# Fused attention and feed-forward kernel: q and k of a head pair normed into one tile and transposed on the chip, with a new model behind the order of instructions

## The chip, the cores and the metric

The kernel runs on one core of a Trainium2 chip. The metric is device time in microseconds (us), from the first to the last instruction of the slowest core (here the only one) as timed without a profile. A profile of one execution is read beside it. Its engines are PE (TensorE matmul), PEld (TensorE weight load), DVE (VectorE), ACT (ScalarE), POOL (GpSimd) and SP (SyncE, which only issues DMA here).

## The reference

Two parts, one after the other. First an attention with RMS-normed q and k (8 batches, 12 heads, 448 positions, head dimension 64), then a feed-forward with the activation h * erf(softplus(h)):

```python
batch, n_heads, seq, head_dim = (8, 12, 448, 64)
def rmsnorm(x, g):
    rms = np.sqrt(np.mean(x * x, axis=-1, keepdims=True) + 1e-06)
    return x / rms * g
q_n, k_n = (rmsnorm(q, g_q), rmsnorm(k, g_k))
scores = (1.0 / np.sqrt(64)) * np.matmul(q_n, k_n.transpose(0, 1, 3, 2))
attn = softmax(scores)                      # over the last axis
attn_out = np.matmul(attn, v)
x = attn_out.transpose(0, 2, 1, 3).reshape(8 * 448, 768)
h = x @ w_in                                # 768 x 2048
sp = softplus(h)
out = (h * erf(sp)) @ w_out                 # 2048 x 768, float32 result
```

(The softmax and softplus are written out in the original; inputs and output are float32.)

## The kernel before

Heads are handled in pairs (two heads of 64 make 128 partitions), six pairs per batch, 48 in all. The kernel does not issue instructions as it goes. It collects operations in a list (`add(engine, cost, due, function, reads, writes, ...)`), orders them by a small model of the engines (`Plan.order`), and emits them in that order. Engines take their own instructions strictly in that order on the chip. The engine letters are P (TensorE), V (VectorE), A (ScalarE), G (GpSimd) and S (SyncE); "VA" means whichever of the two the model finds free.

The path of q and k, batches 1 to 7: load a unit of 4 heads, square on GpSimd, sum on VectorE, 1/rms on ScalarE, scale by it on VectorE to bf16, store to DRAM, and read back transposed, one pair at a time:

```python
    qn_d = [dram.tile([S, d_model], BF16, name=f"qn{b}") for b in range(B)]
    kn_d = [dram.tile([S + D, d_model], BF16, name=f"kn{b}") for b in range(B)]
    ...
    def add_norm(b, a_key):
        for g, units in enumerate(((0, 1, 2, 3), (4, 5, 6))):
            ...
                add("G", 1.5, tg + i, ... nc.gpsimd.tensor_tensor(sq, raw, raw, op=ALU.mult) ...)
                add("V", 0.95, tg + i, ... nc.vector.tensor_reduce(ss[:, i, :], sq, axis=AX.X, op=ALU.add) ...)
            ...                                     # ACT: Ln, then Exp(-0.5 x)
                add("V", 0.96, tg + 8 + i, norm, ... writes=[("qkn", m)])
                for dst, src, dks in unit_stores(qkn, b, u):
                    add("S", 0.5, tg + 10 + i, ... nc.sync.dma_start(dst, src), reads=[("qkn", m)], writes=dks, ...)
    ...
    def add_pair_inputs(b, p):
        if b or p >= N_PET:                         # N_PET = 2
            for nm, dst, src in (("kT", kTs[m], kn_d), ("qT", qTs[m], qn_d)):
                add("S", 1.3, t0 - 14, ... nc.sync.dma_start(
                    dst, src[b][:, p * P : (p + 1) * P], transpose=True), ...)
            def scale():
                nc.vector.tensor_scalar_mul(kps[kp][0:D, 0:S], kTs[m][0:D, D : S + D], gcomb[0:D])
                nc.vector.tensor_scalar_mul(kps[kp][D:P, S : 2 * S], kTs[m][D:P, 0:S], gcomb[D:P])
            add("V", 0.7, t0 - 6, scale, ...)
```

Batch 0 is normed pair by pair; its first two pairs are transposed by TensorE (14 transposes of 128 x 128 in all) and the other four go through DRAM as well. `kp` holds the two heads' scaled keys in the two halves of the partitions, with zeros in the other half, so that a score matmul over all 128 rows gives one head's scores. Attention of one pair: seven score matmuls of 448 columns, four exponentials, eight value matmuls into one PSUM tile `o` with two halves, then Ln, Ln and Exp for the reciprocal of the sum, and two multiplies into `xT`:

```python
    o_ps = ps.tile([P, 2, 512], F32, name="o")
    ...
    add("P", 0.189, ... nc.tensor.matmul(st[:, i, :S], kk[:, c0 : c0 + P], qq, start=True, stop=True) ...)
    add("A", 0.925, ... nc.scalar.activation(e, st[:, :, :S], func=FN.Exp) ...)
    add("P", 0.189, ... nc.tensor.matmul(o_ps[:, half, :S], lhs, rhs, start=(s == 0), stop=(s == 3)) ...)
    ...
    add("V", 0.62, ... nc.vector.tensor_tensor(x[0:D, p, :], o_ps[0:D, 0, :S], r[0:D], op=ALU.mult) ...)
    add("V", 0.62, ... nc.vector.tensor_tensor(x[D:P, p, :], o_ps[D:P, 1, :S], r[D:P], op=ALU.mult) ...)
```

The feed-forward of a batch follows while later batches are in attention: the first product (`f <- xT, w_in_sb`, 96 matmuls of 448 columns, copied to `h` by VectorE or ScalarE), then on ScalarE a block of four Softplus and four Erf with three loads of function tables, then the products h * erf on VectorE, then the second product (`f <- g, w_out_sb`, 96 or 128 matmuls of 384 columns). The block of batch b-1 stands behind all of ScalarE's attention work of batch b:

```python
    for b in range(B):
        if b:
            add_ffn1(b - 1)
        for p in range(NP):
            ...                                     # attention of pair p, inputs of pair p + 1
        if b > 1:
            add_ffn2(b - 2)
        if b:
            add_act_block(b - 1, act_ops(i0))
    add_ffn1(B - 1); add_ffn2(B - 2); add_act_block(B - 1, []); add_ffn2(B - 1)
```

Of the kernel before, what the change touches and what calls it, by code (L numbers as in the profile page):

```python
# [10 lines left out]
F32 = mybir.dt.float32  # L11
# [6 lines left out]
class Op:  # L18
    __slots__ = ("eng", "cost", "lat", "work", "due", "fn", "idx", "need", "users", "ready", "start", "end", "took", "sync", "inst")


class Plan:
# [5 lines left out]
    SLACK = {"P": 0.3, "V": 0.15, "A": 0.1, "G": 0.2, "S": 0.2}  # L28
# [4 lines left out]
    def add(self, eng, cost, due, fn, reads=(), writes=(), lat=0.0, after=(), work=0.0, sync=()):  # L33
# [3 lines left out]
        o.sync = sync  # L37
# [19 lines left out]
    def order(self):  # L57
        free = {e: 0.0 for e in self.SLACK}
        avail = {e: [] for e in self.SLACK}
        future = [(0.0, o.idx) for o in self.ops if not o.need]  # L60
        heapq.heapify(future)
        now, out, dma, lanes = 0.0, [], {}, ([], [])
        while len(out) < len(self.ops):
            while future and future[0][0] <= now + 1e-9:
                o = self.ops[heapq.heappop(future)[1]]
                for i, e in enumerate(o.eng):
                    heapq.heappush(avail[e], (o.due if i == 0 else 1e9 + o.due, o.idx))
            for e, h in avail.items():
                while h and self.ops[h[0][1]].took:
                    heapq.heappop(h)  # L70
                if h and free[e] <= now + 1e-9:
                    o = self.ops[heapq.heappop(h)[1]]
                    o.took, o.start = e, now
                    o.end = now + (o.cost if type(o.cost) is float else o.cost[e])
                    if o.work:
                        done = lanes[e == "G"]
                        if len(done) >= 8:
                            o.end += max(0.0, done[-8] - now)
                    free[e] = o.end
                    out.append(o)  # L80
                    there = o.end
                    if o.work:
                        t0 = max(dma.get(e, 0.0), o.end)
                        busy = max([0.0] + [t for e2, t in dma.items() if e2 != e]) - t0
                        there = dma[e] = t0 + o.work + min(o.work, max(busy, 0.0))
                        done.append(there + o.lat)
                    for u in o.users:
                        u.need -= 1
                        gap = o.lat + (0.0 if u.eng == e and not o.lat else self.SLACK[u.eng[0]])
                        u.ready = max(u.ready, there + gap)  # L90
                        if not u.need:
                            heapq.heappush(future, (u.ready, u.idx))
            nxt = [free[e] for e, h in avail.items() if h and free[e] > now + 1e-9]
            if future:
                nxt.append(future[0][0])
            if len(out) < len(self.ops):
                now = max(now + 1e-6, min(nxt))
        return sorted(out, key=lambda o: (o.start, o.idx))
# [3 lines left out]
def kernel(  # L102
# [26 lines left out]
    dram = ctx.enter_context(tc.tile_pool(name="dram", bufs=1, space=bass.MemoryType.DRAM))  # L129
# [6 lines left out]
    N_RAW, N_SQ, N_QKN, N_ST, N_QT, N_KP, N_V = 4, 1, 2, 2, 3, 2, 4  # L136
    N_VL, N_E, N_EM, N_R, N_X, N_H, N_O = 2, 5, 2, 2, 2, 5, 3
# [4 lines left out]
    raws = ring(sb, N_RAW, [P, 12, D], F32, "raw")  # L142
    sqs = ring(sb, N_SQ, [P, 12, D], F32, "sq")
    sts = ring(sb, N_ST, [P, 4, 12], F32, "st")
    qkns = ring(sb, N_QKN, [P, 12, D], BF16, "qkn")
    s0s = ring(sb, N_ST, [P, 14], F32, "s0")
    qTs = ring(sb, N_QT, [P, S], BF16, "qT")
    kTs = ring(sb, N_QT, [P, S + D], BF16, "kT")
    kps = ring(sb, N_KP, [P, 2 * S], BF16, "kp")
    vms = ring(sb, N_V, [P, 3, 3 * D], BF16, "vm")  # L150
    vls = ring(sb, N_VL, [P, 2, 3, D], F32, "vl")
    vss = ring(sb, N_VL, [P, D], F32, "vs")
# [6 lines left out]
    sps = ring(sb, NC, [P, 4, S], F32, "sp")  # L159
    gms = [ring(sb, NC, [P, 4, 384], BF16, f"g{i}_") for i in range(2)]  # L160
# [5 lines left out]
    o_ps = ps.tile([P, 2, 512], F32, name="o")  # L166
    f_ps = ring(ps, 2, [P, 512], F32, "f")
    qn_d = [dram.tile([S, d_model], BF16, name=f"qn{b}") for b in range(B)]
    kn_d = [dram.tile([S + D, d_model], BF16, name=f"kn{b}") for b in range(B)]
# [3 lines left out]
    PAIR, BATCH = 9.0, 54.0  # L173
# [4 lines left out]
    for half in range(2):  # L178
        for j, g in enumerate((g_q, g_k)):
            add("G", 0.6, -60, lambda half=half, j=j, g=g: nc.gpsimd.dma_start(  # L180
                ggtmp[half * D : (half + 1) * D, j : j + 1], g[:, None]), writes=[("gg", half, j)], lat=2.0)
    add("V", 0.1, -10, lambda: nc.vector.scalar_tensor_tensor(
        out=gcomb, in0=ggtmp[:, 0:1], scalar=8.0, in1=ggtmp[:, 1:2], op0=ALU.mult, op1=ALU.mult),
        reads=[("gg", a, c) for a in range(2) for c in range(2)], writes=["gcomb"])
    for i in range(N_KP):
        add("V", 0.15, -9, lambda t=kps[i]: nc.vector.memset(t[0:D, S : 2 * S], 0.0), writes=[("kp0", i)])
        add("V", 0.15, -9, lambda t=kps[i]: nc.vector.memset(t[D:P, 0:S], 0.0), writes=[("kp1", i)])
    for i in range(N_V):
        def ones(vm=vms[i], vx=vxs[i]):
            nc.vector.memset(vm[:, :, D : 2 * D], 1.0)  # L190
            nc.vector.memset(vx[0:D, 0, D:P], 1.0)
            nc.vector.memset(vx[D:P, 0, :], 0.0)
            nc.vector.memset(vx[0:D, 1, :], 0.0)
            nc.vector.memset(vx[D:P, 1, 0:D], 1.0)
        add("V", 0.5, -8, ones, writes=[("v1", i)])
    add("G", 1.0, -50, lambda: make_identity(nc, ident), writes=["ident"])
    add("A", 1.3, FIRST, lambda: nc.scalar.preload_act_table_set(LN_EXP), writes=["table"])
# [7 lines left out]
    def unit_loads(t, b, u):  # L205
        if u == 0:
            return [(t[0:D], q[b, :, 384:448, :].rearrange("h p d -> p h d")),
                    (t[D:P], k[b, :, 384:448, :].rearrange("h p d -> p h d"))]
        src, h0 = (q, k)[(u - 1) % 2], (u - 1) // 2 * 4
        return [(t.rearrange("p (h j) d -> p h (j d)", j=3),  # L210
                 src[b, h0 : h0 + 4, 0:384, :].rearrange("h (p j) d -> p h (j d)", j=3))]

    def unit_stores(t, b, u):
        t = t.rearrange("p a d -> p (a d)")
        if u == 0:
            return [(qn_d[b][0:D], t[0:D], [("qn", b, 0, hg) for hg in range(3)]),
                    (kn_d[b][0:D], t[D:P], [("kn", b, 0, hg) for hg in range(3)]),
                    (kn_d[b][S : S + D], t[D:P], [("kn", b, 2, hg) for hg in range(3)])]
        dst, nm, hg = (qn_d, kn_d)[(u - 1) % 2], ("qn", "kn")[(u - 1) % 2], (u - 1) // 2
        return [(dst[b][D:S, hg * 256 : hg * 256 + 256].rearrange("(j p) c -> p j c", p=P),  # L220
                 t.rearrange("p (j c) -> p j c", j=3), [(nm, b, 1, hg)])]

    nu = [0]

    def add_norm(b, a_key):
        for g, units in enumerate(((0, 1, 2, 3), (4, 5, 6))):
            tg = BATCH * (b - 1) + 15 * g + (15 if b == 1 else 0)
            si = nu[0] % N_ST
            nu[0] += 1
            ss, n = sts[si], len(units)  # L230
            sks = [("st", si, i) for i in range(n)]
            def bufs(u):
                i = 7 * b + u
                return i % N_RAW, i % N_SQ, i % N_QKN
            for i, u in enumerate(units):
                r, m, _ = bufs(u)
                raw, sq = raws[r], sqs[m]
                rks = [("raw", r, part) for part in range(2)]
                for part, (dst, src) in enumerate(unit_loads(raw, b, u)):
                    add("S", 0.5, tg - 15 + i, lambda dst=dst, src=src: nc.sync.dma_start(dst, src),  # L240
                        writes=rks[part : part + 1] if u == 0 else rks, lat=1.6, work=0.9 if u == 0 else 1.3)
                add("G", 1.5, tg + i, lambda sq=sq, raw=raw: nc.gpsimd.tensor_tensor(  # L242
                    sq, raw, raw, op=ALU.mult), reads=rks, writes=[("sq", m)])
                add("V", 0.95, tg + i, lambda sq=sq, ss=ss, i=i: nc.vector.tensor_reduce(  # L244
                    ss[:, i, :], sq, axis=AX.X, op=ALU.add), reads=[("sq", m)], writes=[sks[i]])
            add("A", 0.34, tg + 6, lambda ss=ss, n=n: nc.scalar.activation(
                ss[:, :n, :], ss[:, :n, :], func=FN.Ln, bias=eps_bias, scale=1.0),
                reads=["eps", a_key], writes=sks)
            add("A", 0.25, tg + 6, lambda ss=ss, n=n: nc.scalar.activation(
                ss[:, :n, :], ss[:, :n, :], func=FN.Exp, scale=-0.5), reads=[a_key], writes=sks)  # L250
            for i, u in enumerate(units):
# [349 lines left out]
```

## Time and profile before

The median of 3 runs is 543.08 us (541.21 to 543.22). The profiled execution has a span of 542.4 us.

| | busy us | share of the span | instructions |
|---|---|---|---|
| VectorE | 367.2 | 68% | 597 |
| ScalarE | 385.8 | 71% | 495 |
| GpSimd | 154.8 | 29% | 219 |
| weight loads on TensorE | 237.3 | 44% | 2,398 |

| groups of instructions | count | busy us | mean ns |
|---|---|---|---|
| exponentials of 128 x 896 (ScalarE) | 144 | 125.4 | 910 |
| squares of 128 x 768 (GpSimd) | 49 | 73.6 | 1,502 |
| sums of squares (VectorE) | 49 | 46.6 | 952 |
| scaling of q, k by 1/rms (VectorE) | 49 | 50.4 | about 1,040 |
| scaling of transposed keys into kp (VectorE) | 92 | 39.5 | about 430 |
| cast of v into vm (GpSimd) | 48 | 35.5 | 739 |
| DMA transposes, time to landing (median) | 46 + 46 | | 3,900 and 3,400 |

How to read the views. The page's second part cuts the span into 40 slices; each digit is the busy share in tenths, PEclk is the clock granted to TensorE in tenths of full speed, and DMA the mean busy share of 16 DMA engines. A row of busy time by stage begins with the stretch and its length in us, then gives the busy us and the number of instructions of PE, PEld, DVE, ACT and POOL in this order, then the granted clock, the DMA share and GB/s moved. A row of waits reads: engine, what it writes and its line, the releaser, then total us, times and the longest. A row of the chain of waits gives start and duration in us and what ran. Ends of matmuls are modelled in the profile, so counts of matmuls say more than PE's busy time.

### The profile page before, as it was taken

What the parts mean: (1) busy time and instruction counts of PE and PEld (TensorE: products, weight loads), DVE (VectorE), ACT (ScalarE), POOL (GpSimd) and SP (SyncE); (2) the same over time, 40 slices, a digit from 0 to 9 for tenths busy, and PEclk for the clock granted to TensorE, in tenths of its full rate; (3) what the DMA queues carried; (4) which work ended last, traced back from release to release, by engine and by line L of the source; (5) the groups of instructions that cost most, each with busy time, mean ns of one, the idle gap of its engine ahead of it and who ended that gap; (6) DMA issues with size and microseconds to landing.
All of it is one profiled execution on the core that took longest, in us unless ns stands there. A gap on an engine that the chain in (4) does not pass through costs nothing.

```text
span 542.4 us, 7384 instructions
## 1 busy us (share of the span) xinstructions
PE 463.0 (85%) x2398; PEld 237.3 (44%) x2398; DVE 367.2 (68%) x597; ACT 385.8 (71%) x495; POOL 154.8 (29%) x219
## 2 busy tenths in 40 slices
PE   0566479966599979799998999989999999999997
PEld 0222134422245534345454544445445545555564
DVE  6654457556798878874988698976876684356621
ACT  3645457849587798569976897779778977796700
POOL 3525246444235322532143313430242020000000
PEclk9955689977799999999999999999999999999999
DMA  6999779999637853974178906683465210110122
GB/s 165 230 171 194 168 173 226 206 182 220 113 100 189 198 126 86 201 197 143 40 157 185 231 24 155 162 211 105 115 146 154 81 27 10 45 73 1 59 73 74
DMA packets 140022, 73.45 MB, mean 135 GB/s; under 512 B 75664, under 2 KB 139216, under 8 KB 139984
## 3 DMA queue, kind: packets, MB, share of 16 engines
q1 hardware_dynamic: 135984, 66.23, 50.9%
q0 software_dynamic: 3168, 6.29, 8.0%
q10 hardware_dynamic: 832, 0.46, 0.3%
q8 instruction: 19, 0.31, 0.3%
q14 instruction: 19, 0.16, 0.1%
HBM read 45.61 MB, written 22.32 MB: 125 GB/s over the span
## 4 chain that ended last, share of the span: by engine, by line
PE 41%; ACT 17%; DMA 14%; DVE 12%; SPq 9%; issue 4%; POOL 2%; DVEq 0%; POOLq 0%
PE f L512 13%; PE f L463 13%; PE o L416 9%; PE s L398 6%; ACT sp L481 5%; ACT sp L477 5%; DMA kn<-qkn 3%; DMA kT<-kn 3%; DVE qkn L258 2%; DVE xT L432 2%; DVE h L450 2%; SPq L374 2%; DMA raw<-in_q_dram 2%; SPq L360 2%; DMA sp<-in_k_dram 2%
## 5 line engine op out<-in xcount | busy, mean ns | idle before, releaser
L463 PE MATMUL f<-xT,w_in_sb 128*128 128x448 bf16 x768 | 171.5, 362 | 15.9 <-DVE h L450 11.5
L404 ACT ACTIVATE e<-s 128x896 bf16<-128x896 f32 x144 | 125.4, 910 | 34.2 <-PE s L398 33.8
L512 PE MATMUL f<-w_out_sb,g 128*128 128x384 bf16 x768 | 130.8, 326 | 0.0
L463 PEld LDWEIGHTS <-w_in_sb 128*128 128x128 bf16 x768 | 76.8, 100 | 94.7 <-issue 30.0
L398 PE MATMUL s<-qT,kp 128*128 128x448 bf16 x336 | 101.7, 380 | 13.5 <-DMA qT<-qn 5.2
L416 PE MATMUL o<-e,vm 128*128 128x448 bf16 x288 | 84.8, 380 | 30.9 <-DVE xT L432 23.1
L512 PEld LDWEIGHTS <-g 128*128 128x128 bf16 x768 | 75.1, 98 | 51.8 <-issue 0.6
L242 POOL TENSOR_TENSOR sq<-raw 128x768 f32<-128x768 f32 x49 | 73.6, 1502 | 82.0 <-DMA raw<-in_k_dram 28.2
L376 POOL CAST vm<-vl 128x384 bf16<-128x384 f32 x48 | 35.5, 739 | 165.8 <-PE o L416 95.0
L450 DVE COPY h<-f 128x448 f32<-128x448 f32 x106 | 65.0, 618 | 24.6 <-PE f L463 23.9
L450 DVE COPY ob<-f 128x384 f32<-128x384 f32 x53 | 29.4, 555 | 53.1 <-PE f L512 48.9
L244 DVE TENSOR_REDUCE st<-sq 128x12 f32<-128x768 f32 x49 | 46.6, 952 | 25.9 <-POOL sq L242 25.1
L492 DVE TENSOR_TENSOR g<-h,sp 128x768 bf16<-128x768 f32 x64 | 59.4, 953 | 0.0
L416 PEld LDWEIGHTS <-vm 128*128 128x128 bf16 x288 | 28.9, 103 | 68.3 <-issue 38.0
L398 PEld LDWEIGHTS <-kp 128*128 128x128 bf16 x336 | 34.0, 103 | 51.1 <-issue 12.6
L477 ACT ACTIVATE sp<-h 128x1792 f32<-128x1792 f32 x32 | 52.0, 1686 | 5.9 <-DVE h L450 5.8
L424 ACT ACTIVATE r<-o 64x448 f32<-64x448 f32 x48 | 26.0, 541 | 39.7 <-PE o L416 36.0
L481 ACT ACTIVATE sp<-sp 128x1792 f32<-128x1792 f32 x32 | 51.7, 1686 | 0.1
L258 DVE TENSOR_TENSOR qkn<-raw,st 128x768 bf16<-128x768 f32 x42 | 43.6, 1055 | 11.8 <-DMA kn<-qkn 7.2
L411 ACT ACTIVATE em<-s 128x448 bf16<-128x448 f32 x48 | 26.1, 544 | 22.1 <-PE s L398 21.4
L430 DVE TENSOR_TENSOR xT<-o,r 64x448 bf16<-64x448 f32 x48 | 29.4, 612 | 15.9 <-ACT r L428 15.6
L381 POOL CAST vx<-vs 64x64 bf16<-64x64 f32 x96 | 33.1, 345 | 19.0 <-DMA vs<-in_v_dram 11.4
(49 smaller groups left out, 317.3 us busy)
## 6 DMA issues: line engine op xcount, KB each, us to landing
vl<-in_v_dram SPq DMA_DIRECT2D x48, 192.0 KB, 3.1
out_dram<-ob SPq DMA_DIRECT2D x48, 192.0 KB, 2.0
raw<-in_q_dram SPq DMA_DIRECT2D x21, 384.0 KB, 4.7
raw<-in_k_dram SPq DMA_DIRECT2D x21, 384.0 KB, 4.6
qn<-qkn SPq DMA_DIRECT2D x21, 192.0 KB, 4.1
kn<-qkn SPq DMA_DIRECT2D x21, 192.0 KB, 3.1
w_in_sb<-in_moe_w_in_dram POOLq DMA_DIRECT2D x6, 512.0 KB, 6.3
w_out_sb<-in_moe_w_out_dram POOLq DMA_DIRECT2D x8, 384.0 KB, 6.3
```

What stands on the lines that cost most here:

```text
L242: add("G", 1.5, tg + i, lambda sq=sq, raw=raw: nc.gpsimd.tensor_tensor(sq, raw, raw, op=ALU.mult), reads=rks, writes=[("sq", m)])
L244: add("V", 0.95, tg + i, lambda sq=sq, ss=ss, i=i: nc.vector.tensor_reduce(ss[:, i, :], sq, axis=AX.X, op=ALU.add), reads=[("sq", m)], wri ...
L258: nc.vector.tensor_tensor(dst, raw.rearrange("p (h j) d -> p h j d", j=3), w.rearrange("p (h j) d -> p h j d", j=3), op=ALU.mult)
L398: add("P", 0.189, t0 + s - 1, lambda st=st, i=i, c0=c0: nc.tensor.matmul(st[:, i, :S], kk[:, c0 : c0 + P], qq, start=True, stop=True), rea ...
L404: add("A", 0.925, t0 + s, lambda e=e, st=st: nc.scalar.activation(e, st[:, :, :S], func=FN.Exp), reads=[("s", sl, 0), ("s", sl, 1), a_key] ...
L416: add("P", 0.189, t0 + s + 0.5, lambda s=s, half=half, lhs=lhs, rhs=rhs: nc.tensor.matmul(o_ps[:, half, :S], lhs, rhs, start=(s == 0), sto ...
L450: nc.vector.tensor_copy(dst, src)
L463: add("P", 0.189, 1e4 + BATCH * (b + 1) + f, lambda f=f, kt=kt, fp=fp: nc.tensor.matmul(fp[:, :S], w_in_sb[:, kt, f * P : (f + 1) * P], x[ ...
L477: last = add("A", 1.68 + (1.28 if c == 0 else 0), -1e3, lambda c=c, ci=ci: nc.scalar.activation(sps[c], hs[ci], func=FN.Softplus), reads=[ ...
L481: add("A", 1.68 + (1.28 if c == 0 else 0), -1e3, lambda c=c: nc.scalar.activation(sps[c], sps[c], func=FN.Erf), writes=[("sp", c, 1), "tab ...
L492: add("V", 0.95, -1e4 + b, lambda h=h, s=s, gm=gm, a=a: nc.vector.tensor_tensor(gm[:, a], h[:, a, D:S], s[:, a, D:S], op=ALU.mult), reads= ...
L512: add("P", 0.162, 1e4 + BATCH * (b + 2.5) + ti, lambda src=src, col=col, nt=nt, js=js, fp=fp: nc.tensor.matmul(fp[:, :JS], src[nt // 4][:, ...
```

## The change

It is a rewrite of how q and k come to TensorE, with a new model for the order. What it is for: to keep the normed q and k on the chip and to bring each instruction and each DMA into an order[...].

- **One tile, one transpose.** q and k of a pair are normed into one tile `qk` (128 x 7 x 128: three blocks of q, one with the last 64 positions of both, three of k). One DMA from SBUF to SBUF transposes all seven blocks. The scratch tensors in DRAM and their stores are gone. 4 of 7 blocks are normed on VectorE and 3 on GpSimd.
- **Keys scaled on GpSimd.** kp is made by three GpSimd products per pair instead of two VectorE operations.
- **First 8 pairs on TensorE.** Their seven blocks are transposed by TensorE and copied out of PSUM (q times the gains); their scores use 64 rows of the array per head, so no zero-filled kp is needed (8 score matmuls instead of 7).
- **Unused products.** 20 matmuls at the start and 36 in batch 0 write a PSUM tile that nobody reads, so that TensorE is active.
- **Two output tiles.** The value matmuls' two halves are two PSUM tiles.
- **Loads.** Batch 0's q and k are loaded into one large area in a few DMAs; the last 64 rows of v come for a whole batch at once; w_in is loaded by groups of 512 columns, one group per attention pair from the first; w_out from pair 9 on, two groups per pair.
- **Order.** The model now keeps a DMA ring per issuing engine with packets and a time per packet, and stretches VectorE and GpSimd operations that would meet on the shared port. Costs and due times are set anew.
- **Buffers.** raw is 2 tiles of 4 heads of q and k (before 4 of 12 blocks), r one (before 2), e four (before 5), v tiles three (before 4); one h chunk of batch 1 lies in g's space.

```diff
-    SLACK = {"P": 0.3, "V": 0.15, "A": 0.1, "G": 0.2, "S": 0.2}
+    SEM = 0.04
...
+        rings, dma_now, lanes = {e: [] for e in "SAG"}, 0.0, ([], [])
...
+                if e == "V" and o.port:
+                    both = shared["G"] - now
+                    if both > 0:
+                        took += both if o.port == "fast" else min(0.75 * took, 0.43 * both)
...
-    N_RAW, N_SQ, N_QKN, N_ST, N_QT, N_KP, N_V = 4, 1, 2, 2, 3, 2, 4
-    N_VL, N_E, N_EM, N_R, N_X, N_H, N_O = 2, 5, 2, 2, 2, 5, 3
+    N_RAW, N_QK, N_ST, N_QT, N_KP, N_V = 2, 2, 2, 4, 2, 3
+    N_VL, N_E, N_EM, N_R, N_X, N_H, N_O = 2, 4, 2, 1, 2, 5, 3
...
-    o_ps = ps.tile([P, 2, 512], F32, name="o")
+    o_ps = ring(ps, 2, [P, 512], F32, "o")
-    qn_d = [dram.tile([S, d_model], BF16, name=f"qn{b}") for b in range(B)]
-    kn_d = [dram.tile([S + D, d_model], BF16, name=f"kn{b}") for b in range(B)]
...
+    def add_norm(b, p):
+        for x, (eng, g, cost) in enumerate((("V", slice(0, 4), 0.7), ("G", slice(4, 7), 0.74))):
+            e = nc.vector if eng == "V" else nc.gpsimd
+            add(eng, cost, tg - 27.29, lambda e=e, g=g: e.tensor_tensor(
+                qks[qi].rearrange("p g h d -> p h g d")[:, :, g], raw[:, :, g],
+                w[:, :, g, None].to_broadcast((P, 2, g.stop - g.start, D)), op=ALU.mult), port="two", ...)
+
+    def add_transposes(b, p):
+        add("S", 1.25, t0 - 27.29, lambda: nc.sync.dma_start(
+            qT.rearrange("p (s t) -> p s t", t=P), qk.rearrange("p g h d -> p (g h d)"), transpose=True), ...)
+        for i, (r, c0, s0, w, c) in enumerate(((0, 0, S + D, JS, 0.75), (0, JS, S, D, 0.14), (D, S, S, S, 0.86))):
+            ...
+                    nc.gpsimd.tensor_tensor(dst, src, g.to_broadcast((D, w)), op=ALU.mult)
...
+                if split:                                        # n < N_PE = 8
+                    dst, lhs, rhs = (st[:, i, :S], qT[r, S + D + s * P : S + D + s * P + P], qq[r]) if s < 3 else (
+                        st[r, 0, :S], qT[r, S : S + D], qq[r])
...
+        if not b:
+            for s in range(3):
+                for i in range(2):
+                    add_idle_product(t0 + s + 0.4, p % 2, qT, ("qT", m))
...
+    def add_w_in(c, sync):
+        f = slice(c * 512, c * 512 + 512)
+        return add("G", 0.8, -20 + 5 * c, lambda: nc.gpsimd.dma_start(
+            w_in_sb[:, :, f], moe_w_in[:, f].rearrange("(kt p) f -> p kt f", p=P)), ...)
...
-                    add("P", 0.162, 1e4 + BATCH * (b + 2.5) + ti, ...      # second product
+                    add("P", 0.1617, 1e4 + BATCH * (b + 2.88) + ti, ...
```

## The prediction, made before the changed kernel ran

> **What bounds the kernel now.** I read the page first: engine totals, then the slices.
>
> ```profile
> PE 463.0 (85%) x2398; PEld 237.3 (44%) x2398; DVE 367.2 (68%) x597; ACT 385.8 (71%) x495; POOL 154.8 (29%) x219
> ...
> PE   0566479966599979799998999989999999999997
> ...
> PEclk9955689977799999999999999999999999999999
> DMA  6999779999637853974178906683465210110122
> ```
>
> TensorE is the busiest, but its row shows two kernels: a ragged first quarter, in which the granted clock also drops to 0.5 to 0.8 and the DMA row is near full, and a dense rest. Next I asked for busy time by stage, cutting at the first score and then at the end of each ScalarE block of the first feed-forward half (Softplus, Erf):
>
> ```profile
> 17.26:75.60 58.34, 34.04 (x103) 12.55 (x104) 29.09 (x49) 30.62 (x52) 23.88 (x29) 0.71 0.94 192
> 75.60:141.00 65.40, 49.60 (x214) 22.25 (x214) 42.80 (x66) 48.60 (x63) 31.47 (x48) 0.87 1.08 204
> 141.00:202.50 61.50, 55.60 (x289) 28.73 (x289) 50.55 (x77) 45.95 (x58) 20.30 (x26) 0.95 0.60 141
> ...
> 377.90:432.80 54.90, 53.66 (x292) 28.18 (x291) 40.73 (x69) 46.62 (x59) 13.64 (x21) 1.00 0.47 123
> ```
>
> Read the instruction counts of the first pair, not its busy time: 103, 214 and 289 matmuls in stages that are as long as the later one with 292. The first three stages have no engine at its limit; their DMA share is 0.94, 1.08 and 0.60. What they wait for is in the chain in order of time and in the waits up to 75 us:
>
> ```profile
> 50.05 8.76 DMA kn<-g
> 58.88 1.16 SPq L360
> 60.13 5.15 DMA qT<-qn
> 65.31 1.65 PE s L398 x4
> ```
>
> ```profile
> PE f L275 <- DVE g L328: 12.9, 2, 12.3
> ACT e L404 <- PE s L398: 12.7, 7, 4.0
> ...
> PE o L416 <- DVE xT L432: 9.7, 3, 5.8
> ...
> DVE kp L364 <- DMA kT<-kn: 7.5, 3, 3.8
> ...
> PE s L398 <- DMA qT<-qn: 5.2, 3, 3.7
> ```
>
> One normed pair takes 15.3 us (50.05 to 65.31) from store to score, through DRAM and back. So: a latency and DMA bound early, TensorE late.
>
> **How much TensorE work there is.** In undisturbed runs of the chain, 96 matmuls of 448 columns take 18.23 us (0.190 each) and 224 of 384 columns take 36.41 us (0.1625). There are 768 + 336 + 384 = 1,488 of the first and 896 of the second: 282.7 + 145.6 = 428.3 us. Of the 542.4 us, 114 are therefore idle or cold time. The last attention ends at 471.1 us (start of the seventh ScalarE block), and the order of the program then leaves 96 + 316 matmuls, 18.2 + 51.4 = 69.6 us, which took 71.3. The tail is TensorE alone. The time is thus decided by when attention of the last batch ends. Attention ends at about 74.6 us for batch 0 (last multiply into xT), then at 124.1, 185.6, 245.5, 302.4, 361.1, 416.0 and 471.1.
>
> **What the Trainium skill says.**
> - "DMA: Bandwidth & Descriptors", section "Two DMAs through the same engine are not ordered": a transfer that reads what another wrote must wait for its completion. The trace agrees: a store into kn takes a median 3.8 us to land and the transpose that reads it another 3.9.
> - "TensorE: Matmul & The Clock Gate", Part 1: without activity the array runs at half clock. The trace agrees: four score matmuls take 1.65 us at 65.31, about 0.4 each, against 0.19 when dense.
> - "TensorEngine Tiling (Array Packing)", "Key Properties": 64-row halves are independent tiles. Nothing in the trace before shows it; I count no gain from it.
> - "SBUF — State Buffer", "Who interferes with whom": a two-input VectorE operation and a GpSimd one that reads SBUF lock each other out. The trace fits: the cast into vm takes 493 ns at best and 2,600 at worst, and its mean is 739.
>
> **The change part by part.**
> *DRAM round trip.* It removes 83 stores of normed q and k (63 in batches 1 to 7, 20 small ones in batch 0); HBM writes fall by the 22.32 - 11.0 MB that aren't output, 11.3 MB. DMA time before: 59.4% of 542.4 = 322 us of all 16 engines. Late in the trace, where transposes run almost alone (436 to 452 us), four of them use 0.13 to 0.15 of four 4 us stretches: 0.56 us each, 52 us for 92. The weight queue takes 8.0%, 43 us. What is left, 227 us, moved about 55 MB: 4.1 us per MB. The stores cost some 46 us, mostly in the crowded first 200 us. Forty transposes replace 92; each moves 229 KB, where two moved 246 KB, so I put it at 1.1 us of DMA, 44 in all. Their SBUF source is the one DMA cost I have no row for.
> *VectorE.* Off it go the 92 scalings into kp (39.5 us), 3/7 of the norms (50.4 to about 42 x 0.70 = 29) and the memsets: about 62 us less, to some 305.
> *GpSimd.* It gets them. From 1,467 ns for a 768-element product, 1.9 ns per element: norm 384 elements 0.75, scalings 384 + 64 + 448 elements 1.8 us with starts. With the square (1,668 for 896 elements), the cast 0.74 and two small casts of 0.345, a pair costs 5.6 us against a pair time of 9. Total about 250 us, from 155. Beside other work.
> *ScalarE.* Twelve more transposed copies of 0.52, fewer squares: +5 us, in the first stage.
> *TensorE.* 42 more transposes (about 5 us), 8 more scores (1.5), and 56 products whose output is not used, in time that is idle anyway; they are there to hold the clock. The two output halves become two tiles, so the next pair need not wait for both multiplies (23.1 us of waits on L432 in the whole trace).
>
> *Batch 0.* First score before: 17.26. After, the chain is: data at 5.6 (as before), square 0.95, reduce 1.08, Ln and Exp 0.50, norm of 896 elements 1.1 (0.96 for 768), seven transposes 1.0, two copies 1.04, and gaps: 12.5. ScalarE then has per pair 3 x 0.91 + 0.54 + 0.54 + 0.54 + 0.58 + 2 x 0.52 + 0.51 = 6.5 us; six pairs at 90% use are 43.3 us. **Attention of batch 0 ends at 56 instead of 74.6.**
> *Batch 1.* The order has 175 matmuls (33.3 us) up to its end; ScalarE has 6 x 4.9 + 1.5 = 31. With a crowded DMA I take 41 us (before 49.5): **97 instead of 124.**
> *Later batches.* From the order, the TensorE work between ends of attention is 49.9, 48.8, 50.6, 52.6, 52.1 and 52.7 us; before it was 42.8, 50.7, 52.9, 53.5, 52.9 and 52.0 in 61.5, 59.9, 56.9, 58.7, 54.9 and 55.1 us. ScalarE needs 49.7 (attention 29.5, norm 1.6, block 17.2, copies 1.4). At the 95.5% that TensorE already reached in the last intervals, and no quicker than ScalarE at 95%: 54 + 52.5 + 53 + 55 + 54.5 + 55 = 324 (before 347). **421.**
> *Tail.* 96 + 328 matmuls: 18.2 + 53.3 + 2.3 of slack = 73.8. **Sum 494.8**, and 0.7 for the distance from span to time (542.4 to 543.08): 495.5, say 496.
>
> **Rivals.**
> *DMA stays the bound early.* By the end of attention 1, some 10 MB of q, k and v (41 us), w_in (21), part of w_out (10 to 20) and first transposes (5) must have moved: 77 to 87 of 97 us. For it: shares of 0.94 and 1.08 before. Against: the stores are gone and the order places each load. If it binds, batches 0 to 2 take 10 to 20 us longer: 506 to 516.
> *GpSimd becomes the bound.* 5.6 us per pair alone; with lockouts as bad as the cast's mean (1.4 times its best) nearly 8 of 9 us, and now keys wait for it, with only two kp buffers. It would show in middle batches at 57 us as before: about 515.
> *A transpose from SBUF is slow*, say twice my figure: 44 us more DMA, hidden in late batches where the share is 0.5; a delay of a few us at each of the first transposed pairs: 500 to 505.
> *Better than thought.* If intervals close to the TensorE work (98%) and batch 0 ends at 53, the end is near 480.
> *A gain that is swallowed*: the tail can't, as TensorE is full there; only an in-order stall from a wrong model would make it as slow as before.
>
> **Range and chances.** The sum has three soft terms: batch 0 (53 to 61), batch 1 (37 to 50) and six intervals (each -1.5 to +2.5). Together 478 to 518 for 8 of 10. For faster by over 2% it need only be under 532, that is keep under a third of the gain: 0.92. Within 2%: 0.05. Slower: 0.03, for a queue order that fits the chip badly.
>
> **What would show it.** First score near 12.5 us and a clock above 0.9 in batch 0; no kn or qn transfer; ScalarE blocks starting near 97, 151, 204, 257, 312, 366 and 421 us; VectorE near 305 and GpSimd near 250 us busy; DMA about 276 us in all; waits of PE for kp short. The prediction is wrong if scores wait for GpSimd's kp or for the transposes into qT, if GpSimd's scaling takes much over 0.9 us for 448 elements, if the DMA row stays at 9 beyond 100 us, or if late intervals stay at 57.

## The result, and the profile after

The changed kernel takes 498.58 us (median of 4 runs, 495.66 to 499.15) against 542.14 us for the kernel before in the same comparison: a ratio of 0.9188, with a 95% interval of 0.9142 to 0.9233. The prediction was 496 (478 to 518).

First the page of the changed kernel, the same rows as shown of the one before: engine totals, then three rows of the 40 slices.

```profile
PE 463.4 (93%) x2504; PEld 241.3 (49%) x2504; DVE 332.0 (67%) x456; ACT 387.0 (78%) x515; POOL 281.5 (57%) x393
...
PE   5968799798999899999999999999999999999997
...
PEclk9697899998999999999999999999999999999999
DMA  8967968985497218840586147721942010210222
```

TensorE's busy time is what it was (463.4 against 463.0, with 106 more instructions); the span around it is 46 us shorter. The last digit under 8 (before the last slice) stands in slice 8 instead of slice 20, and from slice 15 on the row is all nines. The DMA row is still high, 6 to 9, in the first nine slices.

Busy time by stage of the changed kernel (stretch and length, then PE, DVE, ACT and POOL among the five engines, granted clock, DMA share, GB/s): batch 0 from its first score to its last value matmul, then on to the start of ScalarE's first Softplus block, the next interval, and the last one. From 99.97 on the cuts are at the starts of these blocks; the rows of the kernel before were cut at their ends, some 17 us later, so shares and clocks can be compared across the two, lengths not.

```profile
13.05:60.40 47.35, 37.01 (x184) 14.75 (x184) 28.55 (x32) 34.87 (x66) 34.42 (x43) 0.79 0.90 183
60.40:99.97 39.57, 36.18 (x180) 16.59 (x181) 25.23 (x35) 30.61 (x52) 31.56 (x47) 0.97 0.87 161
99.97:157.16 57.19, 54.04 (x281) 27.83 (x280) 44.48 (x59) 46.97 (x61) 42.35 (x56) 0.96 0.75 149
...
369.31:422.35 53.04, 52.85 (x295) 28.65 (x294) 29.82 (x47) 46.97 (x60) 16.64 (x28) 1.00 0.19 51
```

In the last line TensorE has no room left: its work in that interval is 52.7 us of 53.04. Batch 0's attention ends later than the first cut, with its last multiply into `xT`, the event that the prediction counts; it ends at 64.05:

```profile
63.42 0.63 DVE L478 TENSOR_TENSOR xT<-o,r 64x448 bf16<-64x448 f32 x1
```

Waits of TensorE in the whole trace, the longest five (what waited, for whom, total us, times, longest), and the longest of the kernel before:

```profile
PE s L440 <- ACT qT L340: 5.6, 3, 3.5
PE s L440 <- ACT e L446: 4.4, 5, 1.5
PE f L516 <- DVE h L321: 4.0, 8, 1.6
PE f L516 <- ACT h L323: 3.0, 4, 2.0
PE o L462 <- DVE xT L476: 2.7, 5, 0.8
```

```profile
PE o L416 <- DVE xT L432: 23.1, 21, 5.8
```

The 23.1 us of `o` waiting for the second multiply into `xT` are gone (2.7 us are left, for the first multiply). The 12.9 us at the start and the 11.5 us of `f` for VectorE's copies of `h` became 3.8 and 4.0; the waits for ScalarE (`e`, and `h` in its copies) grew, from 1.3 and 0.4. All waits of TensorE in this view add up to 28.6 us, before to 74.8: the difference is as large as that of the spans.

### The profile page after: what moved, and what is told of

The parts are those of the page before. It is cut to its first block, busy times and chain, and to the rows that moved or that the text cites. A ratio compares the mean times of both kernels' runs of the same rounds, so it can differ in the third digit from the quotient of the medians.

```text
span 496.0 us, 7313 instructions
## 1 busy us (share of the span) xinstructions
PE 463.4 (93%) x2504; PEld 241.3 (49%) x2504; DVE 332.0 (67%) x456; ACT 387.0 (78%) x515; POOL 281.5 (57%) x393
## 3 DMA queue, kind: packets, MB, share of 16 engines
HBM read 45.61 MB, written 11.01 MB: 114 GB/s over the span
## 4 chain that ended last, share of the span: by engine, by line
PE 68%; DVE 11%; POOL 7%; issue 6%; ACT 5%; DMA 2%; SPq 0%; POOLq 0%; DVEq 0%; ACTq 0%
PE f L566 26%; PE f L516 20%; PE o L462 12%; PE s L440 8%; POOL sq L266 3%; DVE h L321 2%; POOL kp L306 2%; DVE g L546 2%; DVE godd L546 2%; DMA sp<-in_k_dram 2%; ACT e L446 2%; PE f L483 1%; DVE st L268 1%; DVE xT L476 1%; DVE qk L284 1%
## 5 line engine op out<-in xcount | busy, mean ns | idle before, releaser
L306 POOL TENSOR_TENSOR kp<-qT,gcomb 64x384 bf16<-64x384 bf16 (+2 forms) x120 | 90.6, 763 | 66.1 <-PE s L440 59.7
L266 POOL TENSOR_TENSOR sq<-raw 128x896 f32<-128x896 f32 x42 | 71.7, 1708 | 23.5 <-DMA raw<-in_k_dram 12.7
L440 PE MATMUL s<-qT,kp 128*128 128x448 bf16 x280 | 80.6, 354 | 2.1 <-POOL kp L306 2.0
L566 PE MATMUL f<-w_out_sb,g 128*128 128x384 bf16 x384 | 66.6, 326 | 0.6 <-DVE h L321 0.5
L566 PE MATMUL f<-w_out_sb,godd 128*128 128x384 bf16 x384 | 64.2, 326 | 0.0
L268 DVE TENSOR_REDUCE st<-sq 128x14 f32<-128x896 f32 x42 | 45.4, 1082 | 23.8 <-POOL sq L266 23.3
L566 PEld LDWEIGHTS <-g 128*128 128x128 bf16 x384 | 37.6, 98 | 26.9 <-issue 1.1
L566 PEld LDWEIGHTS <-godd 128*128 128x128 bf16 x384 | 37.6, 98 | 25.1
L284 POOL TENSOR_TENSOR qk<-raw,st 128x384 bf16<-128x384 f32 x42 | 43.6, 1048 | 8.5 <-ACT st L273 7.2
L284 DVE TENSOR_TENSOR qk<-raw,st 128x512 bf16<-128x512 f32 x42 | 41.8, 1019 | 5.8 <-ACT st L273 4.6
```

The source lines that it names most:

```text
L266: add("G", 1.72, tg, lambda part=part: nc.gpsimd.tensor_tensor(sq, part, part, op=ALU.mult), reads=ks, writes=["sq"], port="two")
L268: add("V", 1.08, tg, lambda ss=ss, x=x: nc.vector.tensor_reduce(ss[:, 14 * x : 14 * x + 14], sq, axis=AX.X, op=ALU.add), reads=["sq"], wri ...
L284: add(eng, cost, tg - 27.29, lambda e=e, g=g: e.tensor_tensor(qks[qi].rearrange("p g h d -> p h g d")[:, :, g], raw[:, :, g], w[:, :, g, N ...
L306: nc.gpsimd.tensor_tensor(dst, src, g.to_broadcast((D, w)), op=ALU.mult)
L440: add("P", 0.1887, t0 + s - 0.33, lambda dst=dst, lhs=lhs, rhs=rhs: nc.tensor.matmul(dst, lhs, rhs, start=True, stop=True), reads=[("qT", ...
L566: add("P", 0.1617, 1e4 + BATCH * (b + 2.88) + ti, lambda src=src, col=col, nt=nt, js=js, fp=fp: nc.tensor.matmul(fp[:, :JS], src[nt // 4][ ...
```

## The experiments

All runs but two compute the whole reference; the two that leave something out say so. Ratios are to the kernel before, measured beside each run; the changed kernel has 0.9188 (0.9142 to 0.9233). "Ends of attention" are the starts of ScalarE's Softplus blocks, as in the prediction. The order of instructions was computed anew by each kernel's model unless said otherwise, so neighbours of an edit can move too. The 60 us that two expectations give for batch 0 are the end of its last value matmul.

**One output tile again**

```diff
-    o_ps = ring(ps, 2, [P, 512], F32, "o")
+    o_ps = ps.tile([P, 2, 512], F32, name="o")
```

> The changed kernel with its two output halves in one PSUM tile again. New theory (the split is a main part of the gain): 510 to 520 us, with over 15 us of waits of o for xT (2.8 in the changed kernel). Rival (the later place of the value matmuls in the order hides it): 498 to 503 us.

519.68 us, ratio 0.9559 (0.9507 to 0.9611): 21 us of the 44 are lost, as the first expectation has it; the waits of `o` for `xT`, 13.1 us, fall short of its 15. TensorE's waits, first and fifth row:

```profile
PE o L462 <- DVE xT L478: 13.1, 27, 1.4
...
PE o L462 <- ACT r L470: 3.3, 6, 0.7
```

L478 is the multiply that reads the second half; the matmul that waits writes the first. With one tile the program makes it wait for everything that reads the tile, and also for ScalarE's reading of the sums. The waits seen (16.4 us) don't cover all of the 21; TensorE's busy time also is 8 us longer (471.5 against 463.4). The attention ends move to 106.4, 163.0, 220.0, 276.5, 333.8, 389.6 and 445.0, some 56.4 us apart instead of 53.7. So undoing this one item loses nearly half of the gain: in the profiles 6.4 us up to the end of batch 1 and 16.8 us in the five intervals after batch 2, 2 to 4 us in each; the one between took no longer (56.6 against 57.2).

**Two output tiles in the kernel before**

```diff
-    o_ps = ps.tile([P, 2, 512], F32, name="o")
+    o_ps = ring(ps, 2, [P, 512], F32, "o")
```

> The kernel before with its output halves o as two PSUM tiles instead of one, nothing else. In the kernel before TensorE waited 23.1 us in all for the second multiply into xT (L432) before the first value matmul of the next pair, though that matmul writes the half that the first multiply had read. New theory (this wait, inside every interval, and not the DRAM round trip, holds the intervals at 57 to 61 us): 522 to 533 us, and the waits of o for xT fall under 8 us. Rival (the wait only moves to the next link of the chain on ScalarE and VectorE): 538 to 545 us.

534.58 us, ratio 0.9829 (0.9767 to 0.9891): a gain of 8.5 us (6 to 13 by the interval), between the two expectations. The wait did not fall under 8 us; it moved to the first multiply:

```profile
PE o L416 <- DVE xT L430: 14.9, 7, 4.7
```

Seven long waits in place of 21: here the multiply itself comes late. The same edit is worth 8.5 us in one kernel and 21 in the other, so its value depends on what stands behind the wait.

**The kernel before without the DRAM round trip**

```diff
-                for dst, src, dks in unit_stores(qkn, b, u):
+                for dst, src, dks in ():
-                    dst, src[b][:, p * P : (p + 1) * P], transpose=True),
-                    reads=[(dk, b, i, p // 2 if b else p) for i in range(3)], ...)
+                    dst, src[0][:, 0:P], transpose=True),
+                    reads=["scratch"], ...)              # written once, at the start
```

It leaves out the use of the normed q and k: all pairs but the first two are transposed from a constant.

> The kernel before without the stores of normed q and k; its DRAM transposes read a scratch that is written once at the start (so scores of all but the first two pairs come from constants, and the norms' results are read by nobody). It takes the round trip's wait and load out of the earlier order and leaves the rest. My theory (round trip is the main cause early): attention of batch 1 ends at 100 to 112 us instead of 124, total 515 to 528. Rival (order or engine split is the cause): 535 or more.

542.01 us, ratio 0.9908 (0.9824 to 0.9992): at most a small gain. The early half of the expectation held, the late half failed. Attention of batch 1 ended at 111.6 us instead of 124.1 (some 2 us of this are 12 matmuls that the new order left for later, 288 up to there against 300), and then the next intervals took 61.5, 61.4 and 59.7 us. The first two ends, in the trace in order of time (the table load opens ScalarE's block):

```profile
111.55 1.28 ACT L473 ACT_TABLE_LOAD   x1
...
173.09 1.28 ACT L473 ACT_TABLE_LOAD   x1
```

At the end of batch 7 nothing of the 12.5 us was left (470.6 against 471.1): something else held the intervals at about 60 us, so arriving early bought next to nothing.

**Both together in the kernel before**

The two edits above in one kernel; it leaves out the same part.

> The kernel before with two output tiles and without the DRAM round trip (transposes read a scratch written once; so scores of all but two pairs come from constants). If the round trip holds the first 120 us and the one tile holds the intervals after them, the two together bring what neither does alone: 503 to 518 us, attention of batch 1 ended by 108 us and later intervals of 53 to 56. If something else holds the intervals (the number of operations on VectorE, the place of the value matmuls): 528 to 542.

529.01 us, ratio 0.9737 (0.9681 to 0.9794), about the sum of the two (8.5 + 3.4 us by medians would give 531), and thus the second expectation. Attention of batch 1 ended at 107.8, as expected; the intervals stayed at 60.3, 59.2, 58.2, 59.0, 57.9 and 53.9, which was not. Some 30 us of the gain are thus in neither. The ends of attention tell where they lie: in the profiles 8 us up to the end of batch 1 (107.8 against 100.0) and 26 us in the six intervals (348.4 against 322.4), less 4 us in the tail. The summary of the chain of waits, by line, of this kernel from 168 to 402 us and of the changed kernel from 157 to 422 us:

```profile
by line: PE f L508 11.5%; ACT sp L473 11.0%; PE o L412 9.4%; PE s L394 8.9%; ACT sp L477 7.0%; PE f L459 6.6%; DVE qkn L268 6.4%; issue 4.0%; DVE g L488 3.5%; DVE h L446 3.3%; DVE kp L360 3.1%; ACT L473 2.2%; ACT L477 2.2%; DVE kp L361 1.9%
```

```profile
by line: PE f L566 26.6%; PE f L516 21.6%; PE o L462 12.1%; PE s L440 9.2%; issue 6.3%; DVE godd L546 3.2%; DVE h L321 3.1%; POOL sq L266 2.8%; POOL kp L306 2.5%; DVE g L546 2.1%; DVE qk L284 1.5%; DMA vl<-in_v_dram 1.3%; DVE st L268 1.2%; 
```

In the first, ScalarE's Softplus and Erf (L473, L477) and VectorE's norms and scalings (L268, L360, L361) are on the chain; in the second it is TensorE for 70%. The next four runs narrow down which of the remaining differences does that.

**Keys scaled on VectorE**

```diff
-            engs = "GG"[i // 2 :: 2]
+            engs = "VV"[i // 2 :: 2]
```

> The changed kernel with the keys scaled on VectorE (three products by the gains per pair) instead of GpSimd, order computed anew. VectorE takes on 40 x about 1.0 us and gets some 372 of about 500 us busy, GpSimd falls from 281 to some 190. My theory (VectorE's relief is part of the late gain, but the late intervals have TensorE at 98%, so little is left to lose): 499 to 507 us. Rival (VectorE's load set the late intervals before): 510 or more, late intervals of 55 us and over. Other rival (GpSimd as a loaded helper costs more than it gives): under 496.

499.29 us, ratio 0.915 (0.9108 to 0.9191): no difference. VectorE is busy 371.0 us, as much as in the kernel before, and GpSimd 192.4. In the changed kernel VectorE's total load does not hold the late intervals, and GpSimd's is no burden.

**The norm all on VectorE**

```diff
-        for x, (eng, g, cost) in enumerate((("V", slice(0, 4), 0.7), ("G", slice(4, 7), 0.74))):
+        for x, (eng, g, cost) in enumerate((("V", slice(0, 4), 0.7), ("V", slice(4, 7), 0.54))):
```

> The changed kernel with all seven blocks normed on VectorE in two operations, none on GpSimd. It tells whether the norms are long (1.02 and 1.05 us against my 0.70 and 0.75) because the two engines' halves of the norm run at the same time and lock each other out: if so VectorE's operation of 512 elements falls to 0.7 us. Time: 497 to 503 us, as neither engine is the bound late.

501.65 us, ratio 0.9189 (0.9141 to 0.9236): no difference. The reason that I had for long norms is the smaller part of it: with no norm on GpSimd, VectorE's operation of 512 elements takes 916 ns (1,019 in the changed kernel), not 700.

**The earlier order model, and the earlier due times**

```diff
-    SEM = 0.04
+    SLACK = {"P": 0.3, "V": 0.15, "A": 0.1, "G": 0.2, "S": 0.2}
...                                  # and order() as in the kernel before
```

> The changed kernel with its own costs and due times, but put in order by the earlier model (fixed slacks, no packets, no shared port). My theory (the path of q and k is most of the gain): 503 to 515 us, the first two ends of attention within 8 us of those of the changed kernel, 60 and 100. Rival (the order from the DMA and port model is most of it): over 522 us.

```diff
-    PAIR, BATCH, N_PE = 8.59, 55.11, 8
+    PAIR, BATCH, N_PE = 9.0, 54.0, 8
...
-                add("P", 0.1887, t0 + s + 3.21, ...    # value matmuls
+                add("P", 0.1887, t0 + s + 0.5, ...
...
-                    add("P", 0.1617, 1e4 + BATCH * (b + 2.88) + ti, ...
+                    add("P", 0.1617, 1e4 + BATCH * (b + 2.5) + ti, ...
```

> The changed kernel with the due times that the kernel before has for scores, exponentials, value matmuls (0.5 instead of 3.21 behind the start of their pair), reciprocals and the second product (2.5 instead of 2.88 batches behind), and its pair and batch lengths of 9.0 and 54.0; order computed anew by the new model. With two output tiles and no round trip the kernel before came to 529 us, so some 30 us of the gain are elsewhere. If they lie in where attention and the second product stand in the order: 510 to 522 us, with intervals of 56 and more and TensorE waiting for VectorE's copies of h. If they lie in the first batch and in the smaller or fewer operations of the new norm path: 497 to 504 us.

The old model: 503.96 us, ratio 0.9285 (0.9228 to 0.9342). The old due times: 501.04 us, 0.9248 (0.9209 to 0.9286). Both intervals just meet that of the changed kernel, and by the medians 5.4 and 2.5 us hang on either. Their traces show why a better front is not a better end. With the old model, attention of batches 1 and 2 ended at 96.7 and 151.4, with the old due times at 95.0 and 151.0, both ahead of the changed kernel's 100.0 and 157.2. At the end of batch 7 the lead had shrunk to 3 us and to nothing. The 3 us of the old model are no lead either: it had left more work for the tail, as the row of its tail shows beside that of the changed kernel:

```profile
419.21:499.80 80.59, 77.19 (x458) 44.59 (x456) 38.64 (x62) 34.97 (x26) 0.00 (x0) 1.00 0.17 55
```

```profile
422.35:496.00 73.65, 70.04 (x415) 40.31 (x412) 34.62 (x55) 36.53 (x29) 0.00 (x0) 1.00 0.17 57
```

With 458 matmuls against 415 TensorE is busy 7.2 us longer in it, and the tail is 6.9 us longer. An end of attention is worth what it seems only together with the count of matmuls done by then.

**The new model on the kernel before**

Its `order()` and rings in the kernel before, costs and due times unchanged.

> The kernel before with its own costs, due times and transfers, but put in order by the new model's rings (no port terms, as its operations carry none). My theory: 532 to 548 us, that is no gain without the new path. Rival (order is the main part of the gain): under 525.

553.97 us, ratio 1.0142 (1.0086 to 1.0198): the model alone is no gain, rather a small loss, and more than the 532 to 548 us expected. It was given no port terms here, and the due times were set for another model.

**Through DRAM, in the changed kernel**

```diff
-            qT.rearrange("p (s t) -> p s t", t=P), qk.rearrange("p g h d -> p (g h d)"), transpose=True), ...)
+            qk_d[n].rearrange("(g p) c -> p g c", p=P), qk.rearrange("p g h d -> p g (h d)")), ...)
+        add("S", 1.25, t0 - 27.29, lambda: nc.sync.dma_start(qT, qk_d[n], transpose=True), ...)
```

> The changed kernel, but the normed pair is stored to DRAM and transposed from there (40 stores of 229 KB more, the transposes wait for them), with the order computed anew. My theory (round trip, by latency and load): 508 to 522 us, with waits of the key scaling for the transposes of over 10 us in all (2.9 in the changed kernel). Rival 1 (the transposes are asked for some 27 us ahead, so a longer way is hidden, and the stores find room): 498 to 503. Rival 2 (only the DMA load of the stores counts): the same as the kernel with stores that nobody reads.

507.49 us, ratio 0.9326 (0.9287 to 0.9365): 9 us slower than the changed kernel, between the first two expectations. The waits of the key scaling for the transposes rose only from 2.9 to 4.0 us, so it is not latency at that place. All DMA grew from 53.1% of 496.0 (263 us) to 60.9% of 506.7 (309 us). Losses of some 3 us show by the end of batch 1 and 5.6 by that of batch 2. The tail is 4 us longer, with 442 matmuls left for it instead of 415. That the added DMA load causes the losses is likely, but not shown.

**Stores that nobody reads**

```diff
+        add("S", 0.59, t0 - 27.29, lambda: nc.sync.dma_start(
+            qk_d[n].rearrange("(g p) c -> p g c", p=P), still.rearrange("p (g c) -> p g c", c=P)),
+            reads=["still"], writes=[("qkd", n)], ...)
```

> The changed kernel with 40 stores of 229 KB to DRAM from a constant tile beside the transposes from SBUF; nothing waits for them. It adds the load of the round trip without its latency: 9.2 MB at some 4 us per MB, 37 us of DMA, from pair 8 on. If the load is what counts: 504 to 515 us. If latency counts, or if there is room on the DMA engines by then (shares of 0.5 to 0.75 after 100 us): 498 to 502.

527.87 us, ratio 0.9729 (0.9681 to 0.9777), far above both expectations, because the experiment was not what I meant. The stores wait for nothing, so the order put them wherever SyncE was free, from 21 us on, as SyncE's timeline up to 112 us shows (start, length, how many):

```profile
21.01 2.14 SPq L297 DMA_DIRECT2D qkd<-still  x2
24.64 8.75 SPq L297 DMA_DIRECT2D qkd<-still  x5
...
62.58 4.46 SPq L297 DMA_DIRECT2D qkd<-still  x3
67.89 5.14 SPq L297 DMA_DIRECT2D qkd<-still  x6
```

It can't part load from latency in the run above. What it does tell: all 40 stores cost 303 - 263 = 40 us of DMA (57.8% of 524.9), or 1.0 us each; 21 of them were issued up to 112 us, 21 us of DMA, and attention of batch 1 ended at 116.4 instead of 100.0. So 21 us of load came out as a delay of 16 us in a stretch whose DMA share had been 0.87 to 0.90. The stores also held SyncE, five of them for 8.75 us, ahead of loads that stood behind them; the run doesn't part this from the load on the DMA engines. Where a store stands, and not only its bytes, decides what it costs: the same 9.2 MB more written to HBM cost 9 us in the run above and 29 us here.

**Without the unused products**

```diff
-        add("P", 0.19, due, lambda: nc.tensor.matmul(f_ps[fi][:, :S], t[:, 0:P], t[:, :S], ...), ...)
+        add("P", 0.19, due, lambda: None, ...)           # same order, nothing emitted
```

> The changed kernel, in the same order, without the 56 matmuls whose output nobody reads. My theory (batch 0 is set by ScalarE and by the loads, not by TensorE): 498 to 503 us; the clock in batch 0 falls from 0.79 towards 0.6 and the score pairs there take 0.37 us again, which costs at most 0.2 us at each exposed step. Rival (the warm clock is a real part of the gain): 506 us or more, with the end of batch 0's attention moved from 60 to over 66 us.

500.79 us, ratio 0.9196 (0.9136 to 0.9256): no difference. The granted clock from 13 to 60 us is 0.79 with and without them, so it did not fall as expected. Attention of batch 1 ended at 101.3 instead of 100.0.

## Why the prediction was right, and where it was not

**The number and its skeleton.** The sum was built from ends of attention. From batch 1 on they came out close:

| | predicted | measured |
|---|---|---|
| first score | 12.5 | 13.05 |
| attention of batch 0 ends | 56 | 64.05 |
| of batch 1 | 97 | 100.0 |
| of batch 2 | 151 | 157.2 |
| of batches 3 to 7 | 204, 257, 312, 366, 421 | 210.3, 262.4, 316.0, 369.3, 422.4 |
| tail | 73.8 | 73.65 |

That the end of batch 7 is off by only 1 us is in part luck. Batch 0 took 7.7 us more than predicted and ended outside its own range (53 to 61), and the interval from 1 to 2 took 3.2 us more; batch 1 took 5.1 us less (35.9 against 41), and the five late intervals 4.8 us less.

*TensorE's work as the floor* held. Counting the matmuls between two ends of attention in the program's order and multiplying by 0.190 and 0.1625 us gave 52.1 and 52.7 us for the last two intervals; they took 53.3 and 53.0. Five of the six late intervals together were 265.2 us against 270 expected, and interval 1 to 2 was 57.2 against 54. That one was not at the floor, with 49.9 us of work in the order. The tail, TensorE alone, was exact.

*Batch 0* was mis-sized: 51.0 us for six pairs, not 43.3. The term that failed is ScalarE's use, 90% in the sum and 74% from 13.05 to 60.40 (34.87 of 47.35). ScalarE and TensorE waited for each other there (3.5 us of the first row end with the first score itself):

```profile
PE s L440 <- ACT qT L340: 5.6, 3, 3.5
ACT qT L323 <- PE f L331: 4.6, 4, 2.5
ACT r L470 <- PE o L462: 4.1, 4, 2.2
PE s L440 <- ACT e L446: 4.0, 4, 1.5
```

The DMA share is 0.90, but no wait of these two engines or of VectorE in that stretch ended with a DMA; what the DMA load costs there is not shown. With the same loads in another order batch 1 ended sooner, at 95.0 and 96.7. One loss to a DMA shows ahead of the first score:

```profile
2.70 8.32 DMA sp<-in_k_dram
11.09 0.95 ACT sp L371
12.46 0.55 ACT qT L340
13.05 0.56 PE s L440 x2
```

The square of the second pair waits for the last rows of heads 2 to 11, and pair 0's copy out of PSUM, whose transposes had ended at 9.6 us, stands behind it on ScalarE and starts at 11.9.

*DMA.* 263 us in all against 276 estimated. The 276 takes off the stores but leaves out that 44 us of transposes replace 52; with all of its own terms the sum is 268. A store's cost of about 1.0 us per 229 KB (4.4 us per MB) against 4.1 us per MB was right. A transpose from SBUF lands after 3.0 us (median). Its cost on the DMA engines was not measured alone, but at twice the figure of the prediction the total would be 312 us, so the rival of a slow transpose is out. The rival of DMA as the early bound foresaw 10 to 20 us more for batches 0 to 2; they took 6 us more (157.2 against 151), and DMA as the cause of these is not shown. *HBM writes* fell to 11.01 MB, the output alone.

*VectorE and GpSimd* were mis-sized: 332 and 282 us against 305 and 250. The terms are in the groups by shape (count, busy us, mean ns, then idle time before):

```profile
L284 POOL TENSOR_TENSOR qk<-raw,st 128x384 bf16<-128x384 f32 x42 | 43.6, 1048 | 8.5 <-ACT st L273 7.2
L284 DVE TENSOR_TENSOR qk<-raw,st 128x512 bf16<-128x512 f32 x42 | 41.8, 1019 | 5.8 <-ACT st L273 4.6 <-DMA qT<-qk 0.6
L306 POOL TENSOR_TENSOR kp<-qT,gcomb 64x448 bf16<-64x448 bf16 x40 | 40.2, 1006 | 3.0
```

I had 0.75, 0.70 and 0.86. That the sizes were off cost nothing that shows, as neither became the bound: GpSimd's own long waits were for TensorE to release kp (59.7 us in all), and TensorE waited 2.0 us for kp. The rival "GpSimd becomes the bound" is out.

*The clock* was to be above 0.9 in batch 0; it was 0.79 (0.71 before). The unused products are not what sets it, and not what sets the time.

*Smaller slips.* The distance from span to time, put at 0.7 us, compared two executions; in one and the same it is 2.0 us before (542.4 and 544.42) and 2.2 after (496.0 and 498.15). By the prediction's own rule (95.5% of TensorE's 49.9 us of work) the interval from 1 to 2 is 52.3 us, not 54. Staying under 532 us takes a quarter of the gain, not a third. The cast's mean is 1.5 times its best (739 and 493 ns), not 1.4.

**The reasons were weaker than the number.** I read the early stretch as bound by latency and DMA through DRAM, and for the late intervals I took a use of TensorE of 95.5% without saying which item brings it there. The early reading held by half: without the round trip batch 1 of the kernel before ends 12.5 us sooner, of the 24 that the changed kernel gains there. But at the end this is worth 0 to 2% (0.9908, 0.9824 to 0.9992), and putting the round trip back into the changed kernel costs 9 us, little of it as waiting at the keys. VectorE's relief is worth nothing measurable, for the keys and for the norm each taken alone. And the one item that I named without giving it a term, "the two output halves become two tiles", is what 21 us of the changed kernel's gain hang on. The page of the kernel before names it: TensorE waited 23.1 us for the second multiply. A wait of TensorE itself, in a kernel that TensorE bounds, should have had a term in the sum.

**What stays open.** Two tiles and no round trip, put into the kernel before, make 529 us; the changed kernel has 498.6. The remaining 30 us are not the order model alone, not the due times alone, not the keys' or the norm's share on GpSimd alone, and not the unused products. So the cause of the larger part of the 44 us is not shown. What is left are the norm in units of both q and k with one pair normed at a time, the loads and first eight pairs of the front, and the buffers, or several of these changes acting together; these were not tried one by one, and neither were the order model and the due times together.

## What to carry to other kernels

When one engine sets the end, count its work between two fixed events in the program's order and give each of its own waits a term. A wait of that engine for another's read of the same tile, though it writes another half, is removed by giving each half its own tile; what this brings depends on the next wait behind it (8.5 us of a wait of 23.1 in one kernel here, 21 us in the other). Time won ahead of the bound is not time won: three kernels here ended batch 1 3 to 12 us sooner and kept little or none of it. A change of many parts can be predicted well by its bound and still be explained wrongly, so undo its parts one at a time before copying any of them.

## What the runs showed of the hardware that I had not expected

Two matmuls on 64 rows each, one on the upper and one on the lower half of the partitions, run at the same time. The changed kernel's TensorE timeline has a pair of such score matmuls at 31.07 us, the kernel before a pair over 128 rows at 22.88 us, both of 448 columns (start, length, engine, form, count):

```profile
31.07 0.36 PE L440 MATMUL s<-qT 64*128 64x448 bf16 x2
```

```profile
22.88 0.54 PE L398 MATMUL s<-qT,kp 128*128 128x448 bf16 x2
```

One matmul of 448 columns alone takes 0.35 us from start to end; two on separate halves take 0.36, two on all rows 0.54. This agrees with what the Trainium skill says in "TensorEngine Tiling (Array Packing)", section "Key Properties", on tiles that operate independently. I had counted no gain from it. Eight head pairs with three such pairs of matmuls in place of two over 128 rows save by estimate 24 x 0.18 = 4 us of TensorE's time, in a stretch where it was not the bound.
